# Attention and a gated feed-forward on one core: GpSimd leaves VectorE's arithmetic one pair of token blocks earlier

## The chip, the cores and the metric

The kernel runs on one core of one Trainium2 chip. The metric is the device time of one execution in microseconds (us); the time given for a kernel is the median of its runs. Five engines work side by side, each through its own list of instructions in a fixed order: TensorE (PE in the profile; its weight loads are PEld), VectorE (DVE), ScalarE (ACT), GpSimd (POOL) and SyncE (SP), which issues the transfers here. An instruction that waits for a semaphore holds up all that stand behind it on its engine.

## The reference

Softmax attention over pooled keys and values, and behind it a feed-forward layer whose two inner products are multiplied elementwise:

```python
k_p = k.reshape(B, H, Sp, 8, D).mean(axis=3)          # B, H, S, D = 8, 8, 576, 64; Sp = 72
v_p = v.reshape(B, H, Sp, 8, D).mean(axis=3)
scores = np.matmul(q, k_p.transpose(0, 1, 3, 2)) / np.sqrt(D)
scores = scores - np.max(scores, axis=-1, keepdims=True)
attn = np.exp(scores)
attn = attn / (np.sum(attn, axis=-1, keepdims=True) + 1e-09)
x = np.matmul(attn, v_p)  # to (4608 tokens, 512)
out = ((x @ w_a) * (x @ w_b)) @ w_out                  # w_a, w_b: 512 x 1536; w_out: 1536 x 512
```

All of it is in float32.

## The kernel before, in words

**Tiling.** The 4608 tokens are 36 chunks of 128 for the attention, 12 halves of 384 for the feed-forward, and two halves make a pair: six pairs of 768 tokens. The inner width 1536 is cut into 12 blocks of 128, taken two at a time, so a pair has six steps. The list `items` holds the steps in order: items 0 to 7 are the first pair ("n", plain products), items 8 to 13 the second pair, 14 to 19 the third, and so on to 37 ("s", in which seven block products stand for eight, with sums of weight blocks and of token blocks as their operands). From the third pair on the product with `w_out` goes by seven products as well. While one pair is multiplied, the attention of the next pair's chunks runs in between, and at a change of pair the seven token operands (`xB..`, `xT..`) of the next one are made from its rows `xraw` in `prepare`.

**Precision.** Each float32 operand is split in two: ScalarE rounds it (a cast, the high part) and the difference to the original is the low part (`low_part`, line 281 in every profile row). Each product is then three matmuls: high by high, high by low, low by high. So each operand of TensorE costs one ScalarE cast and one subtraction behind it: `hh` (gated products, 128x384), `sum` and `own` (weights, 128x512), `osum` (sums of `w_out` blocks), `wo`, `ql` (queries), `pr` and `rem` (attention weights), `xB`/`xT` (token operands, 128x768).

**Which engine subtracts.** A small scheduler inside the kernel (class `Machine`) writes out the order of every engine while the program is built: it steps through modelled times, and on each free engine issues the waiting operation of lowest rank. Most operations name their engine. Those made by `either` may go to VectorE or to GpSimd, whichever is free first; the scheduler's model lets neither GpSimd nor an operation of VectorE marked `port` start while another such operation runs:

```python
def either(n, issue, ops=1):
    time = {"DVE": dve(n, ops), "POOL": pool(n, ops)}
    if at_item[0] >= ALONE:
        del time["POOL"]
    return {"time": time, "issue": lambda e: issue(engines[e]), "port": True}
```

`at_item[0]` is the item whose inner products are being issued, and `ALONE` is 14, so GpSimd shares this work through the first and second pair. The sites of `either` that matter here are all the `low` subtractions, the sums of weight blocks (`block_sums`, line 584, tile `sums`; `sums_outer`, line 529, tile `rawo`), the scaling of the attention weights (line 958), the product of the two gates (line 1397, tile `h`) and the token differences of `prepare` (line 1099, tiles `xraw` and `T`). VectorE alone takes what reads PSUM: `h` (lines 1385 and 1391), the sums of the output `y` (line 1492), the maxima (line 890) and the small `least` (line 891).

**Marks in time.** Line 1385 occurs once in each item on VectorE, near the item's end. The scheduler wrote 264 VectorE instructions behind that of item 8 up to that of item 14, and 280 behind it up to that of item 20.

Of the kernel before, what the change touches and what calls it, by code (L numbers as in the profile page):

```python
# [84 lines left out]
SUMS_RANK = 320.0  # L85
SPARE = 1

ALONE = 14

MARGIN = 0.5  # L90

# [112 lines left out]
def dve(n, ops=1):  # L204
    return 0.08 * ops + 0.00104 * n
# [6 lines left out]
def pool(n, ops=1):  # L212
    return 0.2 * ops + 0.00214 * n
# [30 lines left out]
def attn_moe_kernel(ctx: ExitStack, tc: tile.TileContext, q, k, v, vr, wa, wb, wo, out):  # L244
# [26 lines left out]
# [4 lines that stand above are left out]
# [1330 lines left out]
```

## Time and profile before

| what | us |
|---|---|
| median of 3 runs (1015.75 to 1017.97) | 1017.22 |
| the profiled execution | 1016.27 |
| its span, first to last instruction | 1014.5 |
| PE busy, with the modelled ends of its matmuls | 968.1 |
| DVE busy | 855.7 |
| ACT busy | 579.5 |
| POOL busy | 168.0 |

Outside the span lie 1.8 us of the profiled execution. A row of busy time by windows gives for each engine the time in which it had an instruction running, with the number of instructions; PEclk is the share of TensorE's full clock that was granted. A row of a timeline is start, duration, engine, line, operation, the tile written and the tiles read, the shape, and in brackets the idle time of the engine before it with what ended it. On VectorE the next instruction can start a little before the one ahead of it is recorded as ended, so starts are closer together than durations say.

### The profile page before, as it was taken

What the parts mean: (1) busy time and instruction counts of PE and PEld (TensorE: products, weight loads), DVE (VectorE), ACT (ScalarE), POOL (GpSimd) and SP (SyncE); (2) the same over time, 40 slices, a digit from 0 to 9 for tenths busy, and PEclk for the clock granted to TensorE, in tenths of its full rate; (3) what the DMA queues carried; (4) which work ended last, traced back from release to release, by engine and by line L of the source; (5) the groups of instructions that cost most, each with busy time, mean ns of one, the idle gap of its engine ahead of it and who ended that gap; (6) DMA issues with size and microseconds to landing.
All of it is one profiled execution on the core that took longest, in us unless ns stands there. A gap on an engine that the chain in (4) does not pass through costs nothing.

```text
span 1014.5 us, 17014 instructions
## 1 busy us (share of the span) xinstructions
PE 968.1 (95%) x5776; PEld 953.0 (94%) x5776; DVE 855.7 (84%) x1681; ACT 579.5 (57%) x1584; POOL 168.0 (17%) x162
## 2 busy tenths in 40 slices
PE   4689999999999897999999999999999999999997
PEld 3589999999999897999999899999999999999996
DVE  7988896589897788769898988989989888968777
ACT  4789896647865565465455475455466555342331
POOL 4331233165345445000000000000000000000000
PEclk9989999999999998999999999999999999999999
DMA  9768855568876876868675696866778666796661
GB/s 311 239 229 280 283 183 191 172 206 279 302 258 237 291 278 228 302 224 313 243 272 193 221 334 222 297 234 213 268 260 311 229 224 208 258 322 239 236 208 63
DMA packets 88342, 250.16 MB, mean 247 GB/s; under 512 B 9856, under 2 KB 17536, under 8 KB 88256
## 3 DMA queue, kind: packets, MB, share of 16 engines
q1 hardware_dynamic: 88256, 249.08, 70.5%
q8 instruction: 46, 0.75, 0.3%
q14 instruction: 40, 0.33, 0.1%
HBM read 197.13 MB, written 51.90 MB: 245 GB/s over the span
## 4 chain that ended last, share of the span: by engine, by line
PE 86%; DVE 9%; ACT 2%; issue 1%; DVEq 0%; ACTq 0%
PE acc L1459 6%; PE acc L1461 6%; PE acc L1460 6%; PE psc L913 5%; PE psXB L1352 4%; PE psXB L1353 4%; PE psXB L1354 4%; PE psXA L1354 4%; PE psXA L1352 4%; PE psXA L1353 4%; PE psYA L1352 3%; PE psYA L1353 3%; PE psYA L1354 3%; PE psYB L1352 3%; PE psYB L1354 3%; PE psYB L1353 3%
## 5 line engine op out<-in xcount | busy, mean ns | idle before, releaser
L1492 DVE TENSOR_TENSOR y<-acc,y 128x384 f32<-128x384 f32 x304 | 165.0, 552 | 26.5 <-PE acc L1461 22.0
L1259 ACT CAST hh<-h 128x384 fp32r<-128x384 f32 x168 | 85.3, 516 | 92.0 <-DVE h L1397 45.5
L281 DVE TENSOR_TENSOR hh<-h,hh 128x384 fp32r<-128x384 f32 x210 | 118.1, 580 | 5.7 <-ACT hh L1306 3.3
L1459 PE MATMUL acc<-hh,wo 128*128 128x384 f32 x336 | 116.5, 347 | 1.9 <-DVE y L1492 1.2
L1460 PE MATMUL acc<-hh,wo 128*128 128x384 f32 x336 | 114.0, 339 | 2.1 <-DVE hh L281 2.0
L1461 PE MATMUL acc<-hh,wo 128*128 128x384 f32 x336 | 113.7, 338 | 0.0
L875 ACT ACTIVATE weights<-psc,least 128x72 f32<-128x72 f32 x240 | 73.8, 330 | 38.3 <-DVE least L891 34.2
L1379 ACT COPY h<-psXA 128x384 f32<-128x384 f32 x90 | 43.2, 480 | 78.2 <-PE psXA L1354 77.6
L913 PE MATMUL psc<-kdiag,qh 128*128 128x144 f32 x320 | 59.4, 286 | 11.5 <-ACT kdiag L653 10.4
L1459 PEld LDWEIGHTS acc<-hh,wo 128*128 128x128 f32 x336 | 63.5, 189 | 4.9 <-DVE y L1492 3.3
L1460 PEld LDWEIGHTS acc<-hh,wo 128*128 128x128 f32 x336 | 63.6, 189 | 2.9 <-DVE hh L281 2.9
L913 PEld LDWEIGHTS psc<-kdiag,qh 128*128 128x128 f32 x320 | 54.4, 204 | 12.4 <-issue 8.0
L1461 PEld LDWEIGHTS acc<-hh,wo 128*128 128x128 f32 x336 | 63.5, 189 | 0.0
L1267 DVE TENSOR_TENSOR h<-h,h 128x384 f32<-128x384 f32 x96 | 52.7, 549 | 0.5
L1003 ACT CAST turned<-ptr 128x512 fp32r<-128x512 f32 x72 | 40.4, 593 | 19.9 <-PE ptr L996 19.7
L875 ACT ACTIVATION_READ_ACCUMULATOR weights<-psc,least 128x1 f32 x240 | 51.6, 215 | 0.0
L818 POOL MEMSET qh<- 128x256 f32 x4 | 1.2, 311 | 296.6 <-PE psc L913 296.6
L1397 DVE TENSOR_TENSOR h<-h,h 128x384 f32<-128x384 f32 x85 | 49.5, 582 | 0.5
L1353 PE MATMUL psXA<-xT,load 128*128 128x384 f32 x144 | 48.6, 337 | 0.8 <-DVE xT L281 0.8
L1352 PE MATMUL psXA<-xT,load 128*128 128x384 f32 x144 | 48.9, 339 | 0.0
L1352 PE MATMUL psXB<-xT,load 128*128 128x384 f32 x144 | 48.5, 337 | 0.0
L1353 PE MATMUL psXB<-xT,load 128*128 128x384 f32 x144 | 48.5, 337 | 0.0
(301 smaller groups left out, 3165.4 us busy)
## 6 DMA issues: line engine op xcount, KB each, us to landing
load<-kept_S SPq DMA_DIRECT2D x96, 512.0 KB, 4.8
load<-kept SPq DMA_DIRECT2D x72, 512.0 KB, 5.1
wo<-kept_outer SPq DMA_DIRECT2D x48, 512.0 KB, 4.5
wo<-kept_outer SPq DMA_DIRECT2D x48, 384.0 KB, 3.9
kept_S<-sum SPq DMA_DIRECT2D x24, 512.0 KB, 3.2
kept_outer<-osum SPq DMA_DIRECT2D x36, 256.0 KB, 3.6
out<-y SPq DMA_DIRECT2D x48, 192.0 KB, 2.2
kept<-sum SPq DMA_DIRECT2D x18, 512.0 KB, 6.7
```

Of the source, the lines that this page charges most:

```text
L281: eng.tensor_tensor(out=lo, in0=src, in1=hi.bitcast(F32), op=ALU.subtract)
L875: nc.scalar.activation(s[:n, h], src[:, h - hs.start], AF.Exp, bias=least[:n, h:h + 1], scale=SCALE, accum_out=z[:n, h:h + 1],)
L913: nc.tensor.matmul(pt[:n, j * hk:(j + 1) * hk], qq[:, g, cs], kd[:, g, w].rearrange("p e s -> p (e s)"), start=(x == 0), stop=(x == len(to ...
L1259: yield on_act(HB, lambda: nc.scalar.copy(e[:, 0], gf[item, src]))
L1267: yield either(HB, lambda eng: eng.tensor_tensor(out=t, in0=ta, in1=tb, op=ALU.subtract))
L1352: nc.tensor.matmul(pt, w[:, 0, mat, c], xo[:, 0, kk], start=(opens and kk == 0), stop=False, **more)
L1353: nc.tensor.matmul(pt, w[:, 0, mat, c], xo[:, 1, kk], start=False, stop=False, **more)
L1354: nc.tensor.matmul(pt, w[:, 1, mat, c], xo[:, 0, kk], start=False, stop=(kk == 1), **more)
L1459: nc.tensor.matmul(pt, w[:, 0], e[:, 0], start=opens, stop=False, **more)
L1460: nc.tensor.matmul(pt, w[:, 0], e[:, 1], start=False, stop=False, **more)
L1461: nc.tensor.matmul(pt, w[:, 1], e[:, 0], start=False, stop=True, **more)
L1492: yield on_dve(HB, lambda: nc.vector.tensor_tensor(out=acc[at], in0=pt, in1=acc[at], op=ALU.add))
```

## The change

`ALONE` is 8 in place of 14: an operation made by `either` while item 8 or a later one is at work goes to VectorE.

```diff
-ALONE = 14
+ALONE = 8
```

Nothing is computed otherwise. What moves follows from the scheduler, which writes all orders anew from item 8 on. In GpSimd's list 69 arithmetic instructions are gone and VectorE's has 69 more (1750 in place of 1681): 41 of 512 elements a partition, 5 of 768, 7 of 384, 11 of 256 and 5 shorter ones. Five of them stand ahead of the mark of item 8, 50 between it and that of item 14 (264 become 314), 14 between it and that of item 20 (280 become 294). The first difference in VectorE's list stands at 233 us of the trace of before, and from about 637 us of it, the end of item 22, all orders are alike again but for numbers of buffers.

GpSimd's list before, at the change from the second to the third pair (`xT`, `xraw` and `T` belong to the third pair's operands, `pr` and `rem` to a chunk of attention):

```order
L281 TENSOR_TENSOR xT_2_4797<-T_4_175_4576,xT_2_4797 128x768
L1397 TENSOR_TENSOR h_65_4775<-h_65_4775,h_64_4771 128x384
L1099 TENSOR_TENSOR xraw_3260<-xraw_3260 128x2x384
L1099 TENSOR_TENSOR xraw_3260<-xraw_3260,T_4_175_4576 128x2x384
L281 TENSOR_TENSOR pr_4709<-weights_77,pr_4709 128x512
L281 TENSOR_TENSOR rem_4710<-weights_77,rem_4710 128x2x32
L818 MEMSET qh_5859 128x4x64
```

and GpSimd's list now, the last arithmetic of the kernel and what follows:

```order
L529 TENSOR_TENSOR rawo_83_2308<-rawo_83_2308 128x256
L281 TENSOR_TENSOR sum_100_2679<-raw_0_76_2207,sum_100_2679 128x512
L529 TENSOR_TENSOR rawo_83_2308<-rawo_83_2308 128x256
L818 MEMSET qh_2826 128x4x64
L818 MEMSET ql_2827 128x4x64
```

GpSimd's last arithmetic is now a sum of weight blocks just ahead of item 8; behind it only clears of query tiles are left.

VectorE's list before at the same change of pair, up to the mark of item 13 (`hh_46` and `hh_47` are operands of the last `w_out` products of the second pair, for which TensorE's list has `acc_s` directly behind the first six matmuls of the third pair):

```order
L1391 TENSOR_TENSOR h_62_4744<-psYA_5_3_4748,h_62_4744 128x384
L734 TENSOR_REDUCE vp_4548<-vraw_5_4743 96x64
L1391 TENSOR_TENSOR h_63_4756<-psYB_5_3_4763,h_63_4756 128x384
L1397 TENSOR_TENSOR h_63_4756<-h_63_4756,h_62_4744 128x384
L281 TENSOR_TENSOR xT_2_4798<-xraw_3260,xT_2_4798 128x768
L281 TENSOR_TENSOR hh_46_4849<-h_65_4775,hh_46_4849 128x384
L281 TENSOR_TENSOR hh_47_4853<-h_63_4756,hh_47_4853 128x384
L1385 TENSOR_TENSOR h_66_4845<-psXB_5_0_4539,h_66_4845 128x384
```

and now, from the same `hh_46` to the third pair's first operand `xB_2_4833`:

```order
L281 TENSOR_TENSOR hh_46_4718<-h_65_4647,hh_46_4718 128x384
L1391 TENSOR_TENSOR h_63_4612<-psYB_5_3_4630,h_63_4612 128x384
L281 TENSOR_TENSOR osum_185_4731<-rawo_169_4448,osum_185_4731 128x2x128 x2
L1397 TENSOR_TENSOR h_63_4612<-h_63_4612,h_62_4575 128x384
...
L1385 TENSOR_TENSOR h_66_4745<-psXB_5_0_4460,h_66_4745 128x384
L281 TENSOR_TENSOR osum_187_4766<-rawo_169_4448,osum_187_4766 128x2x128 x2
L281 TENSOR_TENSOR hh_47_4777<-h_63_4612,hh_47_4777 128x384
L281 TENSOR_TENSOR hh_48_4787<-h_66_4745,hh_48_4787 128x384
...
L281 TENSOR_TENSOR xB_2_4833<-xraw_3364,xB_2_4833 128x768
```

The seven operands of the third pair, of which some were made ahead of `hh_46`, now all stand behind the mark of item 13, and on TensorE the first four of the last eight `w_out` blocks of the second pair (`acc_s`) stand ahead of the third pair's first matmul in place of behind it.

## Rows read from the trace of the kernel before

**Rows 1.** The page: busy time of each engine, granted clock in 40 slices.
```profile
PE 968.1 (95%) x5776; PEld 953.0 (94%) x5776; DVE 855.7 (84%) x1681; ACT 579.5 (57%) x1584; POOL 168.0 (17%) x162
...
PEclk9989999999999998999999999999999999999999
```
**Rows 2.** Windows: length, busy PE, PEld, DVE, ACT, POOL (count), clock, DMA.
```profile
255.20:430.10 174.90, 165.59 (x987) 162.66 (x986) 144.57 (x264) 107.70 (x308) 72.45 (x60) 0.97 0.76 269
430.10:583.70 153.60, 151.29 (x918) 148.97 (x916) 134.75 (x280) 77.96 (x224) 0.56 (x2) 1.00 0.70 245
...
612.00:816.00 204.00, 204.00 (x1257) 203.11 (x1256) 184.77 (x393) 111.31 (x331) 0.57 (x2) 1.00 0.73 254
843.50:864.50 21.00, 21.00 (x122) 21.00 (x121) 20.90 (x39) 11.10 (x20) 0.00 (x0) 1.00 0.65 226
558.00:584.00 26.00, 23.69 (x132) 21.83 (x131) 25.79 (x48) 10.97 (x21) 0.00 (x0) 1.00 0.66 225
```
**Rows 3.** Waits of TensorE, 255 to 430 us: total, times, longest (us).
```profile
PE acc_s L1428 <- DVE hh L281: 5.0, 1, 5.0
...
PE ptr L996 <- ACT pr L970: 1.2, 1, 1.2
PE ptr L996 <- DVE rem L281: 0.9, 1, 0.9
```
**Rows 4.** Timeline of VectorE, 386 to 412 us.
```profile
388.56 0.94 DVE L281 TENSOR_TENSOR xB<-xraw,xB 128x768 fp32r<-128x768 f32 x1
...
392.45 0.54 DVE L1391 TENSOR_TENSOR h<-psXB,h 128x384 f32<-128x384 f32 x1
392.92 0.54 DVE L1391 TENSOR_TENSOR h<-psYA,h 128x384 f32<-128x384 f32 x1
...
395.58 2.57 DVE L281 TENSOR_TENSOR xT<-xraw,xT 128x768 fp32r<-128x768 f32 x1
398.07 3.60 DVE L281 TENSOR_TENSOR hh<-h,hh 128x384 fp32r<-128x384 f32 x2
```
**Rows 5.** Timeline of GpSimd, 390 to 404 us.
```profile
397.29 2.52 POOL L1099 TENSOR_TENSOR xraw<-xraw,T 128x768 f32<-128x768 f32 x1
399.77 1.50 POOL L281 TENSOR_TENSOR pr<-weights,pr 128x512 fp32r<-128x512 f32 x1
```
**Rows 6.** Timeline of TensorE, 394 to 412 us.
```profile
401.73 0.69 PE L1428 MATMUL acc_s<-hh,wo 128*128 128x384 f32 x1 [5.03 <-DVE hh L281]
...
402.54 0.52 PE L1427 MATMUL acc_s<-hh,wo 128*128 128x384 f32 x1
402.86 0.52 PE L1428 MATMUL acc_s<-hh,wo 128*128 128x384 f32 x1
...
407.55 0.34 PE L1428 MATMUL acc_s<-hh,wo 128*128 128x384 f32 x1
407.73 0.34 PE L1429 MATMUL acc_s<-hh,wo 128*128 128x384 f32 x1
```
**Rows 7.** Groups of GpSimd, 231 to 430 us: count, busy us, mean ns, idle before.
```profile
L281 POOL TENSOR_TENSOR sum<-sums,sum 128x512 fp32r<-128x512 f32 x12 | 16.2, 1348 | 29.3 <-ACT sum L571 25.7 <-PE acc_s L1429 2.7 <-DMA o<-kept_ro 0.9
```
**Rows 8.** Groups of VectorE, 231 to 430 us, the same columns.
```profile
L281 DVE TENSOR_TENSOR hh<-h,hh 128x384 fp32r<-128x384 f32 x25 | 18.6, 749 | 2.0 <-ACT hh L1306 1.0 <-ACT hh L1259 0.6
L1397 DVE TENSOR_TENSOR h<-h,h 128x384 f32<-128x384 f32 x16 | 11.6, 725 | 0.1
...
L891 DVE TENSOR_SCALAR least<-m 128x4 f32<-128x4 f32 x14 | 5.6, 398 | 0.5
```
**Rows 9.** Groups of VectorE, 430 us to the end, the same columns.
```profile
L281 DVE TENSOR_TENSOR hh<-h,hh 128x384 fp32r<-128x384 f32 x166 | 87.7, 549 | 1.3 <-ACT hh L1259 1.2
L1397 DVE TENSOR_TENSOR h<-h,h 128x384 f32<-128x384 f32 x69 | 37.9, 549 | 0.4
...
L281 DVE TENSOR_TENSOR pr<-weights,pr 128x512 fp32r<-128x512 f32 x16 | 10.9, 681 | 0.0
...
L891 DVE TENSOR_SCALAR least<-m 128x4 f32<-128x4 f32 x32 | 5.4, 170 | 1.1
```
**Rows 10.** Waits of GpSimd, 231 to 430 us: total, times, longest (us).
```profile
POOL sum L281 <- ACT sum L571: 59.1, 13, 11.9
```

## The prediction

> **What bounds the kernel now.** I read the page first: TensorE has an instruction running for 968.1 of 1014.5 us, VectorE for 855.7 [rows 1]. TensorE sets the time, so the question is where it stands still or runs slowly, and whether VectorE has something to do with it there. The line of the granted clock dips at the start and in the sixteenth slice, 380 to 406 us, and the change can reach only from 233 to 637 us. So I read windows there, cut at VectorE's line 1385 of items 8, 14 and 20 [rows 2]. In the first stretch, the second pair, 174.9 us long, TensorE is busy for 165.6: it idles 9.3 us, at a mean clock of 0.97. In the second, with GpSimd out of the arithmetic, it idles 2.3 us of 153.6 at 1.00, and from 612 to 816 us not at all. The second pair is the one disturbed place in reach.
>
> The table of TensorE's waits says which these are [rows 3]: one of 5.0 us at `acc_s` for VectorE's `hh`, and 2.1 us at `ptr` for ScalarE's `pr` and VectorE's `rem`; what is left is small. The timelines tell the reason of the first. From 395.58 to 401.67 us VectorE ran three subtractions that read two operands from SBUF: one `xT` in 2.57 us and two `hh` in 3.60 together [rows 4]. A like subtraction of 768 elements took 0.94 us at 388.56 [rows 4], one `hh` without GpSimd beside it 549 ns [rows 9]. All the while GpSimd ran `xraw`, for 2.52 us, and `pr`, for 1.50 [rows 5]. Adds that read PSUM kept their 0.54 us beside it [rows 4]. So GpSimd's work of this kind and VectorE's hold each other up, and here the held instruction was the one that TensorE stood waiting for. The stop has a second price. The matmuls behind it start 0.32 us apart, from 407.55 on 0.18 [rows 6]: the lower of the clock's two levels, 1.2 in place of 2.4 GHz, after TensorE had idled. Sixteen matmuls, from 402.2 to 407.2 us, at 0.14 us too much are 2.2 us. So the first stretch holds 9.3 + 2.2 = 11.5 us that a TensorE without stops would not need. That is about the ceiling of the gain there.
>
> **What is added to VectorE.** The moved instructions by size: 41 of 512 elements last 681 ns on VectorE [rows 9], and the next starts about 0.07 us before the recorded end (0.54 us long, 0.47 apart [rows 4]): 41 x 0.61 = 25.0 us. Five of 768 at 0.94 - 0.07 = 0.87: 4.4. Seven of 384 at 0.55 - 0.07 = 0.48: 3.4. Sixteen of 256 or less, by the step from 512 to 384 elements (0.13 us a 128), at most 0.35: 5.6. Together 38.4 us for 69, or 0.56 each. The orders say where they stand: 50 between the marks of items 8 and 14 (27.8 us), 14 up to that of item 20 (7.8 us), 5 ahead.
>
> **What is given back on VectorE.** With GpSimd silent the same instructions shrink from their means in the second pair [rows 8] to those behind it [rows 9]: `hh` 25 x (749 - 549) = 5.0 us, the product of the gates 16 x (725 - 549) = 2.8, `least` 14 x (398 - 170) = 3.2, and the one `xT` 2.57 - 0.94 = 1.6. That is 12.6 us; the smaller groups give some more, so it is a floor.
>
> At GpSimd's price the moved work was worse than this: a `sum` of 512 elements took 1348 ns there [rows 7]. That shortens the way from a cast to its matmul, but I count nothing for it, since TensorE waits for no `sum` of GpSimd in [rows 3].
>
> One rule of the Trainium skill bears on the size (SBUF — State Buffer, "Who interferes with whom"): GpSimd and a VectorE instruction with two SBUF inputs share a port pair under an exclusive lock, and the loser "fully blocks". If every microsecond of GpSimd stopped such work in full, up to the 72.45 us that GpSimd is busy in the stretch would come back; the rows that I could price say 12.6 or somewhat more, and the sum goes by them.
>
> **Does VectorE still fit?** In the first stretch it was busy for 144.6 us [rows 2]. Now 144.6 + 27.8 - 12.6 = 159.8. If TensorE's 11.5 us shrink to some 2.5, the stretch lasts 174.9 - 9.0 = 165.9 us, and VectorE is busy for 0.96 of it. Is that too much? From 612 to 816 us it was busy for 184.8 of 204.0, 0.91, and TensorE did not idle; from 843.5 to 864.5 for 20.9 of 21.0 and TensorE did not idle either; only from 558 to 584, at 25.8 of 26.0, did TensorE lose 2.3 us [rows 2]. VectorE is so near to full there because its queue runs behind; it needs not be early, only not late. At 0.96 it is close to its end, but below it. I keep 2.5 us of stops for this: the 2.3 us that such a full stretch cost, and a little clock.
>
> The worst place should be the change of pair, where VectorE's list now has the whole set of the third pair's operands behind the mark of item 13. But `hh_47`, for which TensorE stood 5.0 us, now stands ahead of all of them, with two short `osum` in front, and TensorE has four blocks of `acc_s` (24 matmuls at 0.18 us, 4.3 us) before it needs the first new operand. If VectorE were late there by more than these 4.3 us, each further one would be TensorE's.
>
> Second stretch: 134.8 + 7.8 = 142.6 us busy of 153.6, 0.93. That is between the share that cost nothing and the one that cost 2.3 us, and the 2.3 us of idle there may go or grow as much. I count it at nothing, within plus or minus 2 us. From 637 us on the orders are alike, so nothing changes. Transfers: SyncE's order follows the scheduler, the DMA share is 0.76 in the stretch [rows 2], and TensorE waits for none in [rows 3]; I count nothing.
>
> **Sum.** 1016.27 - 9.0 = 1007.3 us for an execution like the profiled one; the median of the runs is 0.95 us above it, so 1008.
>
> **Rivals.** *First, slower: the waits move to VectorE's queue.* GpSimd stood idle 59.1 us in 13 waits for ScalarE's casts of `sum` [rows 10]. It could, because nothing that TensorE needs at once stood behind. On VectorE the same subtraction holds up the adds that free PSUM. VectorE has 174.9 - 159.8 = 15.1 us before the stretch becomes longer than it was. Some 38 of the 50 moved instructions follow a cast; if each stands waiting for 0.4 us, the room is used up, and at 0.6 us (22.8 us) the stretch grows by 7.7: 1017.2 + 7.7 = 1025. For it: the 59.1 us, and VectorE's high share. Against: the scheduler issues a subtraction only when its cast is done in its model, and 25 `hh` cost VectorE only 2.0 us of idle [rows 8]; GpSimd's waits show that it had little to do, not that casts come late for a busy queue. The Trainium skill speaks for this rival too (Perfetto Trace Analysis, "Optimizing Scalar/DVE Operations"): a full VectorE may be relieved by GpSimd; it adds itself that between these two it "might not help". By its first half this change goes the wrong way, to the time just given.
>
> *Second, the same or little gain: a new stop in place of the old.* At the change of pair VectorE has seven operands and four differences of 768 elements to make, 11 x 0.87 = 9.6 us, among adds and `hh`. If it comes there late by 9 to 10 us, TensorE's 4.3 us of cover leave a stop like the old one, 5 us, and 2 us of clock: of the 9.0 us about 2 remain, 1015. For it: 0.96. Against: the first operand is needed first, the others follow each two blocks of products apart (2.1 us), more than two of these instructions take.
>
> *Third, more gain.* VectorE keeps up everywhere, and the stop of 558 to 584 us shrinks as well: 11.5 + 2.3 = 13.8, or 1017.2 - 13.8 = 1003.
>
> That the change does nothing is excluded: the lists of the engines differ as told.
>
> **How the numbers follow.** Forecast (1005 to 1012): 0.52. More gain (1000 to 1005): 0.17. Little gain or none (1012 to 1019): 0.15, of which 0.08 lie within 0.2%, some 2 us, which is what a measurement of this kernel can tell from no change. Slower (1019 to 1027): 0.16. So faster 0.76, same 0.08, slower 0.16. The range leaves out most of the slower case and the tip of the better one: 1001 to 1019.
>
> **What would show it.** In the profile after: POOL's row with no arithmetic behind 231 us; VectorE's `hh` and gate product at about 550 ns and `least` at 170 also in the second pair; no TensorE wait over 2 us at `acc_s` near the change of pair, and a clock of 1.00 there; VectorE at 0.93 to 0.97 of the second pair. Wrong would be: TensorE waits for `sum`, `xB` or `xT` of line 281 that add up to more than 5 us, VectorE idle before `sum` with ScalarE as the releaser, or a third pair longer than 155.6 us.

## The result, and the profile after

| | before | after |
|---|---|---|
| median, runs side by side on the same chip (us) | 1016.56 (1015.75 to 1017.97) | 999.05 (998.71 to 999.90) |
| ratio, with its 95% interval | | 0.9828 [0.9811, 0.9845] |
| profiled execution, and its span | 1016.27, 1014.5 | 998.71, 996.9 |

The change saves 17.5 us. The forecast was 1008, a gain of 9, and 999.05 lies below the lower end of the range, 1001: the sign was right, the size was not. One execution of the ten of the run with marked operations below took 2406.24 us and is left out of its time; why it was slow is not known.

The page of the kernel after, its busy times and its rows of 40 slices for GpSimd and for the granted clock:

```profile
PE 960.7 (96%) x5776; PEld 948.7 (95%) x5776; DVE 867.9 (87%) x1750; ACT 580.6 (58%) x1584; POOL 83.3 (8%) x93
...
POOL 4331333161000000000000000000000000000000
...
PEclk9989999999999999999999999999999999999999
```

GpSimd has no arithmetic behind the tenth slice, and the dip of the clock in the sixteenth slice [rows 1] is gone. The windows answer to [rows 2], cut at the same marks (items 8, 14, 20 and 23), with the same columns:

```profile
255.30:414.90 159.60, 158.78 (x969) 157.68 (x968) 150.53 (x315) 104.34 (x296) 0.00 (x0) 1.00 0.79 281
414.90:567.20 152.30, 152.30 (x943) 151.67 (x943) 140.31 (x294) 84.11 (x244) 0.57 (x2) 1.00 0.75 264
567.20:644.50 77.30, 77.30 (x477) 76.94 (x476) 69.17 (x151) 46.42 (x148) 0.00 (x0) 1.00 0.80 285
```

Of the 17.6 us by which the span is shorter, 15.3 lie in the second pair (174.9 to 159.6), 1.3 in the third (153.6 to 152.3), 0.8 in the half pair behind it, and 0.2 elsewhere. All waits of TensorE of 0.2 us and more, from 229 to 600 us, where [rows 3] had one of 5.0 and a pair of 2.1:

```profile
PE po L1045 <- ACT weights L875: 0.8, 1, 0.8
PE psXA L1354 <- DVE sum L281: 0.6, 1, 0.6
PE psXA L1352 <- ACT h L1379: 0.3, 1, 0.3
PE psXA L1352 <- ACT sum L571: 0.2, 1, 0.2
```

The groups of VectorE from 231 to 415 us answer to [rows 8]:

```profile
L281 DVE TENSOR_TENSOR sum<-sums,sum 128x512 fp32r<-128x512 f32 x24 | 16.4, 682 | 0.5 <-ACT sum L571 0.5
L281 DVE TENSOR_TENSOR hh<-h,hh 128x384 fp32r<-128x384 f32 x27 | 14.9, 551 | 0.3
L1397 DVE TENSOR_TENSOR h<-h,h 128x384 f32<-128x384 f32 x21 | 11.6, 552 | 0.0
```

`hh` takes 551 ns instead of 749, the product of the gates 552 instead of 725. VectorE idled 0.5 us in front of 24 `sum`, where GpSimd had idled 59.1 us in front of 13 [rows 10].

**Where TensorE's time was lost, counted from start to start.** The idle time in a row is what lies between the recorded end of one matmul and the start of the next. Timeline of TensorE after, around its longest stop from item 8 to item 20:

```profile
386.07 0.34 PE L1046 MATMUL po<-turned,vdiag 128*128 128x384 f32 x1
386.25 0.35 PE L1047 MATMUL po<-turned,vdiag 128*128 128x384 f32 x1
386.43 0.33 PE L1048 MATMUL po<-rest,vrem 96*128 96x384 f32 x1
387.53 0.44 PE L1045 MATMUL po<-turned,vdiag 128*128 128x384 f32 x1 [0.77 <-ACT weights L875]
```

Starts are 0.18 us apart, so the last matmul was due at 386.61 and came at 387.53: 0.92 us lost, of which the row calls 0.77 idle. A matmul recorded for 0.33 us hides about 0.15 us of each stop. I therefore summed, over all matmuls of a pair, how much later each started than the usual step between two of its sizes (the median over the whole trace):

| lost by starts (us) | second pair before | after | third pair before | after |
|---|---|---|---|---|
| stops that have an idle row | 10.7 (8 stops, 9.3 idle) | 1.1 (2 stops, 0.8 idle) | 3.4 (6 stops, 2.3 idle) | 0 |
| steps at the slower clock | 4.1 (32 steps) | 0 | 0 | 0 |
| small delays, nearly all of 0.15 us or less | 1.5 | 1.4 | 1.2 | 1.1 |
| sum | 16.3 | 2.6 | 4.6 | 1.1 |

So 13.7 us came back in the second pair, nearly all of it stops and clock, and 3.5 in the third, 17.2 together. Of the 4.6 us of the third pair, 4.0 lie between the marks of items 19 and 20, at the change to the fourth pair. The rest of the difference between the stretches is TensorE's own work: by the usual steps 1.5 us of it left the second pair and 2.3 came into the third (918 matmul rows before, 943 after), with fewer in the half pair behind it.

### The profile page after: what moved, and what is told of

Its sections match the earlier page's. It is cut to its first block, busy times and chain, and to the rows that moved or that the text cites. A ratio compares the mean times of both kernels' runs of the same rounds, so it can differ in the third digit from the quotient of the medians.

```text
span 996.9 us, 16951 instructions
## 1 busy us (share of the span) xinstructions
PE 960.7 (96%) x5776; PEld 948.7 (95%) x5776; DVE 867.9 (87%) x1750; ACT 580.6 (58%) x1584; POOL 83.3 (8%) x93
## 4 chain that ended last, share of the span: by engine, by line
PE 89%; DVE 7%; ACT 1%; issue 1%; DVEq 0%; ACTq 0%
PE acc L1459 6%; PE acc L1461 6%; PE acc L1460 6%; PE psc L913 5%; PE psXB L1352 4%; PE psXA L1352 4%; PE psXA L1354 4%; PE psXB L1353 4%; PE psXB L1354 4%; PE psXA L1353 4%; PE psYA L1352 3%; PE psYB L1352 3%; PE psYA L1354 3%; PE psYA L1353 3%; PE psYB L1354 3%; PE psYB L1353 3%
## 5 line engine op out<-in xcount | busy, mean ns | idle before, releaser
L281 DVE TENSOR_TENSOR hh<-h,hh 128x384 fp32r<-128x384 f32 x212 | 114.7, 558 | 5.0 <-ACT hh L1306 2.3
L913 PE MATMUL psc<-kdiag,qh 128*128 128x144 f32 x320 | 59.3, 286 | 11.8 <-ACT kdiag L653 10.7
L913 PEld LDWEIGHTS psc<-kdiag,qh 128*128 128x128 f32 x320 | 54.4, 204 | 12.6 <-issue 8.3
L1352 PE MATMUL psXB<-xT,load 128*128 128x384 f32 x144 | 48.7, 338 | 0.0
L1353 PE MATMUL psXB<-xT,load 128*128 128x384 f32 x144 | 48.4, 336 | 0.0
L1354 PE MATMUL psXB<-xT,load 128*128 128x384 f32 x144 | 48.3, 336 | 0.0
```

The costliest lines, as they stand in the source:

```text
L281: eng.tensor_tensor(out=lo, in0=src, in1=hi.bitcast(F32), op=ALU.subtract)
L913: nc.tensor.matmul(pt[:n, j * hk:(j + 1) * hk], qq[:, g, cs], kd[:, g, w].rearrange("p e s -> p (e s)"), start=(x == 0), stop=(x == len(to ...
L1352: nc.tensor.matmul(pt, w[:, 0, mat, c], xo[:, 0, kk], start=(opens and kk == 0), stop=False, **more)
L1353: nc.tensor.matmul(pt, w[:, 0, mat, c], xo[:, 1, kk], start=False, stop=False, **more)
L1354: nc.tensor.matmul(pt, w[:, 1, mat, c], xo[:, 0, kk], start=False, stop=(kk == 1), **more)
```

## The experiments

Two theories stood against each other. The first is the prediction's: GpSimd's arithmetic held up VectorE, and through it TensorE. The rival: the scheduler wrote a new order from item 8 on, and that order, not GpSimd's silence, brings the gain. All times are medians, 4 runs each if nothing else is said; ratios are to the kernel before on the same chip (1016.2 to 1016.6), with 95% intervals. "Lost" is the count from start to start, in the second and the third pair. The code of a run is shown in part; `...` stands for lines left out.

**The orders of before, with VectorE alone.** The scheduler plans with `ALONE` = 14; only the engine that gets the instruction is another:

```diff
-        return {"time": time, "issue": lambda e: issue(engines[e]), "port": True}
+        late = at_item[0] >= 8
+        return {"time": time, "issue": lambda e: issue(engines["DVE" if late else e]), "port": True}
```

> The scheduler plans as in the kernel before (GpSimd shares until item 14), so the orders of TensorE, ScalarE and SyncE are those of before; only the 69 instructions that it gives to GpSimd from item 8 on are issued on VectorE, at the places where they were issued. Theory 1 (contention: what GpSimd did to VectorE's two-operand instructions cost TensorE its stops): the 5.0 us wait at acc_s and the one at ptr go although the order is the old one; some 12 of the 17.5 us come back, 1002 to 1007 us, with hh and gate product at about 550 ns in the second pair. Theory 2 (order: the gain is that the scheduler wrote a new list, in which the third pair's operands stand behind hh): with the old order nothing is gained, 1014 us or more, since VectorE has some 37 us more to do in lists that were planned without it, and new stops appear.

Measured: 1009.97 us, 0.9939 [0.9924, 0.9953], a gain of 6.6. Its windows, second and third pair:

```profile
257.70:424.40 166.70, 161.99 (x983) 157.78 (x982) 155.52 (x325) 108.51 (x309) 0.00 (x0) 1.00 0.80 280
424.40:578.00 153.60, 151.26 (x917) 149.00 (x915) 134.76 (x280) 77.98 (x224) 0.56 (x2) 1.00 0.71 245
```

and in its timeline of VectorE the `xT` and the two `hh` of [rows 4], there 2.57 and 3.60 us:

```profile
396.51 0.95 DVE L281 TENSOR_TENSOR xT<-xraw,xT 128x768 fp32r<-128x768 f32 x1
397.38 1.02 DVE L281 TENSOR_TENSOR hh<-h,hh 128x384 fp32r<-128x384 f32 x2
```

TensorE's wait for them:

```profile
PE acc_s L1428 <- DVE hh L281: 0.8, 1, 0.8
```

The same three instructions in the same order take 1.97 in place of 6.17 us when GpSimd is silent, TensorE's wait at `acc_s` falls from 5.0 to 0.8 us, and the clock stays at 1.00. So the mechanism of the prediction is there. But it is worth 6.6 us, not 17.5, and the time lies between the ranges that the two theories gave. The second pair still loses 8.5 us (16.3 before), its first mark comes 2.5 us later, and the third pair loses 4.7, as it did before (4.6): there GpSimd's silence does nothing.

**The orders of after, with GpSimd sharing.** The fourth corner. The scheduler plans as after, so the orders of TensorE, ScalarE and SyncE are those of after, and the 69 instructions that GpSimd had before are issued on GpSimd again (`WAS_POOL` lists them by the step that makes them):

```diff
-        time = {"DVE": dve(n, ops), "POOL": pool(n, ops)}
+        time, there = {"DVE": dve(n, ops), "POOL": pool(n, ops)}, key_of(nth) in WAS_POOL
...
-        return {"time": time, "issue": lambda e: issue(engines[e]), "port": True}
+        return {"time": time, "issue": lambda e: issue(engines["POOL" if there else e]), "port": True}
```

> The fourth corner of a square of two by two with the kernel before (old order, GpSimd shares), old order on VectorE alone (1010.0 us) and the changed kernel (new order, VectorE alone, 999 us): the scheduler plans as in the changed kernel, so the orders of TensorE, ScalarE and SyncE are those of the changed kernel, but the 69 instructions that GpSimd had in the kernel before are issued on GpSimd, at their places in the new plan. Theory 6 (two shares that add: contention and the slower engine cost some 7 us whatever the order, the order is worth some 11): 1004 to 1008 us, hh at 650 ns or more in the second pair. Theory 7 (they do not add: the new order, with TensorE's next work standing further off, hides what GpSimd does): 998 to 1002 us, though hh grows as well. Theory 8 (a plan made for VectorE suits GpSimd worse than the old one): 1010 us and above.

Measured: 1006.08 us, 0.9905 [0.9888, 0.9921]. Lost: 7.9 and 1.1 us; the first mark comes 2.2 us later than after. Its second pair, its longest wait of TensorE there, and three groups of VectorE from 231 to 420 us:

```profile
257.50:422.70 165.20, 161.56 (x969) 159.25 (x970) 141.92 (x255) 103.88 (x296) 74.00 (x60) 0.99 0.77 270
```

The wait:

```profile
PE psc L913 <- POOL ql L281: 2.1, 1, 2.1
```

And the groups:

```profile
L281 DVE TENSOR_TENSOR hh<-h,hh 128x384 fp32r<-128x384 f32 x24 | 16.1, 674 | 1.9 <-ACT hh L1306 1.6
L1397 DVE TENSOR_TENSOR h<-h,h 128x384 f32<-128x384 f32 x15 | 11.8, 785 | 0.2
...
L891 DVE TENSOR_SCALAR least<-m 128x4 f32<-128x4 f32 x13 | 5.6, 431 | 0.4
```

VectorE is held up as in [rows 8] (785 and 431 ns beside 725 and 398 there, `hh` 674 beside 749), and yet more than half of the gain, 10.3 of 17.5 us, is there. The four corners, in us:

| | GpSimd shares | VectorE alone | difference |
|---|---|---|---|
| orders of before | 1016.6 | 1010.0 | 6.6 |
| orders of after | 1006.1 | 999.05 | 7.0 |
| difference | 10.5 | 10.9 | |

The two effects add, as far as these times can tell. By the medians GpSimd's sharing costs 6.6 to 7.0 us under either order, and the new order is worth 10.5 to 10.9 us with or without GpSimd. By the ratios, of which each is known to some 1.6 us, the same four differences are 6.2, 7.8, 9.7 and 11.3 us.

**From item 13 on alone, and all but item 13.** The first has `ALONE` = 13, so that GpSimd leaves one item earlier than before; the second leaves item 13 shared:

```diff
-        if at_item[0] >= ALONE:
+        if at_item[0] >= ALONE and at_item[0] != 13:
```

> ALONE is 13 in place of 14: GpSimd is out of the arithmetic only from item 13 on, so at the change from the second to the third pair alone. Theory 1 (contention, summed over places): the stop at the change of pair goes with its slow clock (5.0 + 2.2 us), the stops in items 10 to 12 stay: 1007 to 1011 us. Theory 3 (one place: the change of pair is all of it): 999 to 1003 us. Theory 2 (order): no clear expectation, anything from 1000 to 1020.

> ALONE is 8, but in item 13 GpSimd shares again, as in the kernel before. Theory 1 (contention, summed over places): the items 8 to 12 keep their gain, the change of pair has GpSimd's long instructions beside VectorE's again and a stop of some us with slow clock behind it: 1004 to 1010 us. Theory 3 (one place): nearly all of the gain is lost, 1012 to 1017 us.

Measured: 1004.0 us (1001.77 to 1005.24), 0.9884 [0.9868, 0.9901], and 1001.15, 0.9853 [0.9838, 0.9868]. The first lies between the ranges expected of it, the second below all of its own: the contention of the places, summed up, explains neither. The windows of the second pair, from item 13 on alone:

```profile
255.10:419.90 164.80, 160.87 (x986) 158.55 (x985) 142.48 (x273) 105.67 (x303) 53.65 (x47) 1.00 0.79 279
```

and with item 13 shared:

```profile
255.40:417.80 162.40, 160.88 (x979) 158.52 (x980) 150.13 (x307) 106.70 (x301) 16.95 (x15) 1.00 0.80 281
```

Item 13 alone gives 12.6 us, all but item 13 gives 15.5, both give 17.5: the shares of the items don't add, because each variant gets another order. The profile of the first is of its fastest execution (1001.77 us). It suggests where most of the order's gain sits. With GpSimd still at work for 53.65 us, 6.6 us are lost in the second pair, nearly all of it ahead of item 12. The two items around the change of pair, which lost 6.4 and 2.8 us before, lose 0.1 and 0.5, and the third pair loses 0.8. Once the third pair's operands are planned for VectorE alone, both the change of pair and the third pair run nearly without a stop, in this execution.

**Put GpSimd beside the kernel after.** Thirty-nine casts of a weight sum on ScalarE are each followed by two subtractions on GpSimd, of 192 elements with two operands, whose result nobody reads. The orders of the kernel after are kept; in items 8 to 13:

```diff
+    def copy_and_more(hi, src):
+        nc.scalar.copy(hi, src)
+        for part in [hi[:, j, :192].bitcast(F32) for j in range(2) if 8 <= at_item[0] < 14]:
+            nc.gpsimd.tensor_tensor(out=extra, in0=part, in1=part, op=ALU.subtract)
...
-            yield on_act(512, lambda: nc.scalar.copy(e[:, 0], src))
+            yield on_act(512, lambda: copy_and_more(e[:, 0], src))
```

> The changed kernel with 39 pairs of instructions on GpSimd added in items 8 to 13, whose result nobody reads: behind each ScalarE cast of a weight sum GpSimd subtracts 192 elements of it from themselves, twice (two operands from SBUF). No work is taken from VectorE and the orders of all other engines are those of the changed kernel. Theory 1 (contention): VectorE's two-operand instructions in the second pair grow again (hh from 550 towards 650 to 700 ns), VectorE has some 8 to 10 us more in a stretch of 160 in which it is busy for 150, and TensorE gets stops: 1003 to 1010 us. Theory 2 (order): the order is untouched, 998 to 1001 us.

Then the same with a copy, which reads one operand:

```diff
-            nc.gpsimd.tensor_tensor(out=extra, in0=part, in1=part, op=ALU.subtract)
+            nc.gpsimd.tensor_copy(extra, part)
```

> As the run with idle work on GpSimd (39 pairs of subtractions of 192 elements: 1004.5 us, sum on VectorE at 769 ns in place of 683), but each of the instructions is a copy with one operand from SBUF. If what GpSimd reads holds VectorE up, however many operands it has, sum stays above 720 ns, and the time falls only as far as the copies are shorter: 1000 to 1004 us. If it takes two operands on GpSimd, sum is at 683 ns again: 998 to 1000 us.

Measured: 1004.54 us, 0.9884 [0.9870, 0.9899], so 5.5 us over the kernel after, and 1000.32, 0.9847 [0.9832, 0.9862], 1.3 over it. The added work on GpSimd, and the groups of VectorE: first with subtractions (231 to 420 us),

```profile
L287 POOL TENSOR_TENSOR extra<-sum 128x192 f32<-128x192 f32 x78 | 61.4, 787 | 94.5 <-ACT sum L286 91.0
```

and on VectorE,

```profile
L281 DVE TENSOR_TENSOR sum<-sums,sum 128x512 fp32r<-128x512 f32 x24 | 17.7, 736 | 0.0
L281 DVE TENSOR_TENSOR hh<-h,hh 128x384 fp32r<-128x384 f32 x27 | 15.1, 559 | 0.3 <-ACT hh L1306 0.2
L1397 DVE TENSOR_TENSOR h<-h,h 128x384 f32<-128x384 f32 x21 | 13.2, 630 | 0.0
L281 DVE TENSOR_TENSOR sum<-raw,sum 128x512 fp32r<-128x512 f32 x16 | 12.7, 792 | 0.1
```

then with copies (GpSimd 231 to 420, VectorE 231 to 416 us):

```profile
L287 POOL COPY extra<-sum 128x192 f32<-128x192 f32 x78 | 44.4, 569 | 107.9 <-ACT sum L286 105.4
```

and on VectorE,

```profile
L281 DVE TENSOR_TENSOR sum<-sums,sum 128x512 fp32r<-128x512 f32 x24 | 16.9, 705 | 0.4 <-ACT sum L286 0.4
L281 DVE TENSOR_TENSOR hh<-h,hh 128x384 fp32r<-128x384 f32 x27 | 14.8, 549 | 0.4 <-ACT hh L1306 0.2
L1397 DVE TENSOR_TENSOR h<-h,h 128x384 f32<-128x384 f32 x21 | 12.1, 575 | 0.0
L281 DVE TENSOR_TENSOR sum<-raw,sum 128x512 fp32r<-128x512 f32 x16 | 11.9, 746 | 0.1
```

Work on GpSimd whose result nobody reads slows VectorE's two-operand instructions, and the subtractions cost the kernel time: of the 5.5 us, 2.7 lie in the second pair, and the first mark comes 3.1 later (258.4 us). The 1.3 us of the copies are not clear of the noise, since the intervals of the ratios overlap (0.9832 to 0.9862, after 0.9811 to 0.9845). That the added reads also keep the buffers of `sum` longer was not separated. The `hh` that I had named in the expectation stayed near 550, since 18 of the 27 had no GpSimd instruction beside them (548 ns; the 9 others 581). Of the gate products 10 of 21 ran beside one and took 719 ns on the mean, of `sum<-raw` 11 of 16, at 844. So it depends on what runs at the same time, not on the kind alone.

**Fill VectorE instead.** Forty-two unread subtractions of 192 elements stand on VectorE itself, each behind the low part of a weight sum, in the orders of after:

```diff
+    def low_and_more(n, lo, src, hi):
+        part = hi[:, 0, :192].bitcast(F32)
+        return either(n, lambda eng: [low_part(eng, lo, src, hi)] + [nc.vector.tensor_tensor(out=extra, in0=part, in1=part, op=ALU.subtract)] * (8 <= at_item[0] < 14))
...
-            yield low(512, e[:, 1], src, e[:, 0])
+            yield low_and_more(512, e[:, 1], src, e[:, 0])
```

> The changed kernel with 42 instructions of 192 elements added on VectorE, one behind each subtraction of a weight sum, result unread; some 0.28 us each by the spacing of the others, 11 to 12 us together, nearly all in the second pair, where VectorE is busy for 150.5 of 159.6 us. The orders are those of the changed kernel otherwise. Theory of room (VectorE may be busy for nearly all of a stretch and TensorE not notice): 150.5 + 11.5 = 162, over the length by 2.4 us, and with the 2 to 4 us of idle that the fullest stretches keep the stretch grows by 4 to 7 us: 1003 to 1006 us. Rival (a VectorE above 0.94 stops TensorE by what is added, since each held instruction holds those behind it): the full 11 us or more, 1010 us and above.

Measured: 1003.23 us, 0.9873 [0.9854, 0.9891], 4.2 over the kernel after.

```profile
256.60:419.20 162.60, 160.16 (x969) 157.30 (x967) 158.11 (x349) 103.75 (x295) 0.00 (x0) 1.00 0.78 274
```

VectorE is busy for 158.11 of 162.60 us, 0.97, within 2 us of the prediction's 159.8. TensorE then loses 5.6 us in the pair, 3.0 more than after, and reaches its first mark 1.3 us later. So the fear that VectorE would be too full had a right size, a few microseconds; the kernel after is not in that state, as it has 150.53 of 159.60, 0.94.

**Tell the scheduler of more sharing.** The kernel before, with two more VectorE operations, the maxima with `least` and the inverse sums, marked so that its model does not run them beside GpSimd's:

```diff
-            yield on_dve(2 * hk, greatest, 2)
+            yield on_dve(2 * hk, greatest, 2, port=True)
...
-        yield on_dve(H if late else H * SP, inverse, 2)
+        yield on_dve(H if late else H * SP, inverse, 2, port=True)
```

> The kernel before (ALONE 14), but in the scheduler's model the small instructions behind the maxima (least) and the inverse of the sums are marked as holding the port too, as the trace shows them held (least 398 ns beside GpSimd, 170 without). Theory 4 (the stops come from a plan that does not know what GpSimd really costs): with these marks the plan is nearer to the truth and some stops go, 1008 to 1013 us. Theory 5 (the marks are a small part of it; what is held are mostly instructions that the model knows as held, and GpSimd's long instructions still stand in the way of what TensorE waits for): 1013 to 1019 us.

Measured: 1017.53 us, median of nine executions (1014.32 to 1019.17), 1.0012 [0.9998, 1.0025]: no change. The wait of 5.0 us for `hh` is gone, and 8.7 us are lost in the second pair in place of 16.3, but at the same change of pair TensorE now stands for another instruction of VectorE:

```profile
405.16 0.44 PE L1352 MATMUL psXB<-xB,load 128*128 128x384 f32 x1 [2.46 <-DVE h L1385]
```

The first mark comes at 261.6 us in place of 255.2, and the third pair loses 4.9. Another order alone is not a better one.

**From the first item on, and from item 6.** `ALONE` = 0 and `ALONE` = 6 in place of 8:

> ALONE is 0: GpSimd takes no part in this arithmetic from the start; in the first pair VectorE has 59 instructions more, 1809 in all. If contention is the larger part in the first pair too (VectorE's instructions there grow beside GpSimd as well), another 3 to 8 us: 991 to 996 us. If VectorE's load is the larger part there (the opening has VectorE at 0.8 to 0.9 and ScalarE at 0.9, and TensorE waits for the first operands), slower than the changed kernel: 1002 to 1012 us.

> ALONE is 6: GpSimd leaves with the last two items of the first pair. Those two items are fully busy on TensorE in the trace of the changed kernel (it idles for less than 1 us from 160 to 231 us), so there is nothing to win there but a different list behind: 996 to 1002 us.

Measured: 1002.57 us (1001.14 to 1003.07), 0.9861 [0.9847, 0.9876], and 997.78 (997.06 to 998.11), 0.9818 [0.9801, 0.9834]. Without any sharing (VectorE has 1814 instructions in the trace, not 1809) the mark of item 8 comes 3.2 us earlier than after (252.1 beside 255.3 us), but the item behind the change of pair loses 4.1 us in place of 1.2, and the whole is 3.5 us slower than after. So the time fell into the range that I gave for a VectorE too full in the opening, but not for that reason: the opening is faster, and the loss lies behind it. `ALONE` = 6 is the fastest that I ran, 1.3 us under the kernel after; their executions don't overlap, but the intervals of the ratios do.

## Why the prediction was wrong

**Right: the bound and the mechanism.** TensorE sets the time, VectorE's held-up instructions at the change of pair made it stand, and its clock fell behind that. The run with the old orders shows each of these: 6.17 us of held work become 1.97, the wait of 5.0 becomes 0.8, and the slower clock is gone. The signs that I named came as told: no arithmetic on GpSimd behind 231 us, 551 and 552 ns for `hh` and the gate product, 171 ns for `least`, no wait of TensorE over 0.8 us from 229 to 600 us, a clock of 1.00, and 0.94 of the second pair for VectorE.

**Wrong: the ceiling of 11.5 us.** This is the step that failed first, "9.3 + 2.2 = 11.5 us that a TensorE without stops would not need". By starts it is 16.3. Three parts make up the difference: 1.4 us of the eight stops, which lie inside recorded durations; 1.9 us of slower steps, because a second slow stretch at 332 us was left out. It stands in the timeline of TensorE before, behind the two waits at `ptr` of [rows 3]:

```profile
332.61 0.72 PE L996 MATMUL ptr<-ident,pr 128*128 128x128 f32 x4 [0.92 <-DVE rem L281]
...
333.89 0.52 PE L1354 MATMUL psXA<-xT,sum 128*128 128x384 f32 x1
...
334.21 0.52 PE L1352 MATMUL psXA<-xT,sum 128*128 128x384 f32 x1
334.53 0.52 PE L1353 MATMUL psXA<-xT,sum 128*128 128x384 f32 x1
...
335.96 0.33 PE L1354 MATMUL psXB<-xT,sum 128*128 128x384 f32 x1
336.13 0.34 PE L1352 MATMUL psXB<-xT,sum 128*128 128x384 f32 x1
```

Starts 0.32 us apart up to 335.2, 0.17 to 0.18 from 335.8 on. And 1.5 us of delays too small for an idle row, which the change left as they were. The rival "more gain" had the same ceiling under it, so its 1003 was too high as well.

The second pair can be added up. To the 9.0 us that I forecast come 3.3 of stops and slow steps that the ceiling lacked, 1.4 of stops kept that did not come (below), 0.1 of small delays, and 1.5 of TensorE's own work that the new order has elsewhere: 15.3, as measured. The other 2.3 us of the span lie behind that pair.

**Wrong: the 2.5 us of stops kept for a full VectorE.** After, TensorE's stops in the second pair are 1.1 us. VectorE was forecast at 159.8 us busy and had 150.53. The price of the moved work (27.8 us) stood up in kind: `sum` 682 ns, beside 681 for a like subtraction in [rows 9]. What was mis-sized is what comes back: 144.57 + 27.8 - 150.53 = 21.8 us by that price, an estimate, not the floor of 12.6. Instruction by instruction, against the durations of the same shapes in the trace of after (from 255 us on), the 264 instructions of the second pair were held by 18.0 us: 11.0 in the four groups that I priced (I had counted them from 231 us on, 24 us ahead of the pair), 7.0 in those that I had put down as "some more" (`rem`, `T`, `osum`, `sum`, `z` and others). The 4 us that still lack I cannot place. The lock of the Trainium skill (SBUF — State Buffer, "Who interferes with whom") is borne out in kind and gave no measure: 72.45 us of GpSimd gave back 21.8, 0.30 each, as most of the work did not meet: in the second pair 30 of 120 instructions of VectorE with two operands in SBUF ran beside GpSimd's arithmetic, and 58 of 93 that read PSUM. From 231 to 430 us, 7 of 25 `hh` ran beside it and took 1256 ns on the mean, the 18 others 552.

**Wrong: the third pair at nothing.** It lost 4.6 us and now loses 1.1. The run with the old orders and a silent GpSimd has 4.7 there, that with the new orders and a sharing GpSimd 1.1: it is the order. I had looked at that pair as one whose instructions were given, since GpSimd had no part in it already. But the planner writes all lists anew from item 8 on. Of the 4.6 us, 4.0 are the stop from 558 to 584 us that the third rival named, at the change to the fourth pair. Before, VectorE had made one of the seven operands of the fourth pair at the mark of item 19 (558.9 us), and TensorE came to stand for another:

```profile
554.37 0.95 DVE L281 TENSOR_TENSOR xB<-xraw,xB 128x768 fp32r<-128x768 f32 x1
563.12 0.95 DVE L281 TENSOR_TENSOR xB<-xraw,xB 128x768 fp32r<-128x768 f32 x1
569.31 0.45 PE L1353 MATMUL psXA<-xT,load 128*128 128x384 f32 x1 [0.77 <-DVE xT L281]
```

After, the first starts 18 us ahead of that mark (543.7 us), and the fifth begins ahead of it:

```profile
525.70 0.95 DVE L281 TENSOR_TENSOR xB<-xraw,xB 128x768 fp32r<-128x768 f32 x1
542.81 0.95 DVE L281 TENSOR_TENSOR xT<-xraw,xT 128x768 fp32r<-128x768 f32 x1
```

All twelve kernels fit this: the three with one operand made at the mark (before, the old orders on VectorE, the marked operations) lose 3.9 to 4.0 us in that item, the nine with four or five made at most 0.3. No run moved these operands alone, so that their place is the cause is argued from the traces.

**Not seen: the order as a term of its own.** The working priced instructions that move from one list to another and asked what a fuller VectorE does; of the new lists it looked at the change of pair alone, for a new stop. The 10.5 to 10.9 us of the new order stand in no line of it. What the terms priced, the end of the sharing, measured 6.6 to 7.0 by the medians where I forecast 9.0. So less than half of the 17.5 us comes from what was priced, and that the sign held by so wide a margin is luck.

**The rivals.** Waits moved to VectorE's queue: 0.5 us idle in front of 24 `sum`, so no. The Trainium skill (Perfetto Trace Analysis, "Optimizing Scalar/DVE Operations") says that a saturated VectorE may be relieved by GpSimd, and that between these two it might not help. The trace agrees with the second half: with the orders held, taking the work back gained 6.6 us. Of a saturated VectorE the pair shows nothing, as it was busy for 0.83 of the pair (144.57 of 174.90 us) and for 0.94 after. More gain: its mechanism is the one that came, a VectorE that keeps up everywhere and a stop at 558 us that goes; I gave its range, 1000 to 1005, a chance of 0.17, and 999.05 lies just below it. A new stop at the change of pair: VectorE's timeline after shows why not.

```profile
386.64 0.75 DVE L281 TENSOR_TENSOR osum<-rawo,osum 128x256 fp32r<-128x256 f32 x2
387.31 1.16 DVE L281 TENSOR_TENSOR hh<-h,hh 128x384 fp32r<-128x384 f32 x2
389.60 0.56 DVE L1492 TENSOR_TENSOR y<-acc_s,y 128x384 f32<-128x384 f32 x1 [1.13 <-PE acc_s L1429]
```

Behind the two `hh` VectorE stands waiting for TensorE, not the other way round: it is ahead.

**Open.** Why the planner's new lists leave the change from the second to the third pair without a long stop, where the old ones do not, was not taken apart further than to item 13. The count of operands does not tell it there: before, four of seven were made at the mark of item 13, after, none. Nor is it settled whether `ALONE` = 6 is better than 8 for a reason or by a luckier list; the spread between lists of nearly the same plan (997.8 to 1004.0 us) is larger than the difference between those two.

## What to carry to other kernels

Count what the bounding engine loses from start to start against its usual step, and count every slow stretch: idle rows and the longest wait gave 11.5 us here, the starts 16.3. Where a planner writes the orders, a change of who does the work is two changes, the end of a contention and a new order; run the old order with the new assignment and the new order with the old one before you explain a gain by either. A second engine that was busy for 0.94 of its time left the first one with 1.1 us of stops here; filled up to 0.97 it cost 3.0 us more in the pair, and 4.2 in the whole kernel.

## What the runs showed of the hardware

GpSimd held up VectorE with one operand too. Copies of 192 elements that read one operand, 44.4 us of them, raised VectorE's `sum` from 685 to 746 ns and the gate product from 552 to 575, while the two-operand subtractions (61.4 us) raised them to 792 and 630. The adds that read PSUM kept their time (`y` 550 and 547 ns beside 552). For each microsecond of GpSimd, as recorded, within the pair VectorE was busy 0.07 us longer with copies (150.53 to 153.19 us for 35.94) and 0.12 longer with subtractions (to 156.22 for 49.21), against an estimated 0.30 in the kernel before, whose pieces are up to 768 elements long. That the longer pieces are the reason was not tried.

A mean hides two populations. In the kernel before, from 231 to 430 us, instructions of VectorE that no record of GpSimd's arithmetic overlaps take the same time as in a silent stretch, and the others from half as long again to almost four times as long: gate product 544 ns (10) and 1026 (6), `sum<-sums` 679 (9) and 1038 (3), `hh` as told above; `y`, which reads PSUM, takes 554 (15) and 554 (25). A small instruction can be held for longer than it lasts: `least`, four elements a partition, takes 170 ns alone (7) and 626 beside GpSimd (7), which makes the mean of 398 [rows 8].
